# Attention and FFN in one kernel: the first two chunks take turns in the FFN, three inner tiles each and then thirteen each

## The chip, the cores and the metric

The kernel runs on one core of one Trainium2 chip. The metric is the device time of one execution in microseconds (us); less is better. Engines are named as in the profile: PE is the matrix engine (PEld its weight loads), DVE VectorE, ACT ScalarE, POOL GpSimd, SP SyncE, which here only issues DMAs.

## The reference

Attention over blocks of 32 queries, each seeing 16 keys to its left, 8 to its right and 8 memory keys; its output, with the heads side by side, is the input x of an FFN with 3072 tokens, 512 model columns and 2048 inner units:

```python
scores = scale * np.matmul(q_c, k_full.transpose(0, 1, 3, 2))
a = np.exp(scores - np.max(scores, axis=-1, keepdims=True))
out[:, :, c_start:c_end] = np.matmul(a / (np.sum(a, axis=-1, keepdims=True) + 1e-09), v_full)

h = x @ w_in                      # x: attention's output, (3072, 512)
r = np.maximum(h, 0.0)
g = s * (r * r) + b               # s and b: one number each
return (g @ w_out).astype(np.float32)
```

## The kernel before, in words

The 3072 tokens are cut into 8 chunks of 384. Each chunk has an attention part (4 pairs of heads) and an FFN part of 16 steps, one for each tile f of 128 inner units. A step is `hidden(u)`, 12 matmuls that make h from x (L504), four ACT instructions (relu, square, affine, and the rounded high part gH, L511 to L514), one DVE instruction (the low part gL, L515), and `result(u)`, 9 matmuls that add g times w_out into three PSUM accumulators (L526). x, g and the weights are held as a high and a low fp32r part, so that a product is three matmuls.

The weights come as 64-bit numbers, 512 KB for each of the 32 weight tiles (w_in and w_out, 16 each, "half" 0 and 1). Each is decoded once, in `weight`: ACT scales the upper word (L481), DVE shifts the lower word (L482), joins the two (L484) and puts the sign in (L486), ACT rounds the high part (L490) and DVE subtracts to get the low part (L491). The raw words lie in ten tiles `early0` to `early9`, and after these in a ring `words` of four tiles; the joined number lies in a ring `wv` of three. A tile of `words` can be loaded again once L486 has read it.

One pair of heads in attention: scores (PE, L377), row maxima with the mask (DVE, L434, eight to a pair), exp (ACT, L438, eight), a reciprocal (DVE, L443) and a multiplication (POOL, L444) for each of the two heads, then a turn: for the first two chunks PE transposes (L453) and ACT or DVE copies (L456, L458), for later chunks DVE transposes in 32x32 blocks (L464). The values product (L409) and the two parts of x (ACT L413, DVE L414) end it. Tiles `t` and `aT` are rings of four, two to a pair of heads.

The order of the FFN steps is the list `STEPS`: eight steps of chunk 0 (f 0 to 7), sixteen of chunk 1, the other eight of chunk 0, then chunks 2 to 7. At a change of chunk the three accumulators are put aside (`result`, L537, ACT) and added to later (L544, DVE).

The order on each engine is not written by hand: `Plan.lay` (L140) is a list scheduler over all operations, with a due time for each (a weight: `ORDER`, L50; a pair of heads: `anchor`, L346), a table of durations (`HOLD`), and a model of the DMAs (`RATE`, `LAND`, at most eight in flight). What it lays is the in-order program of each engine; the wait for a late operand holds everything behind it on that engine. While PE has nothing to do in the first 40 us, filler matmuls are laid (L304). s and b are loaded by two small DMAs, one number to each of 128 partitions (L310, L311).

Of the kernel before, what the change touches and what calls it, by code (L numbers as in the profile page):

```python
# [11 lines left out]
F32 = mybir.dt.float32  # L12
# [27 lines left out]
NEG = -2.0 ** 100  # L40
NEARLY = 16
NTURN = 2
N0 = 8
LAG = 2
NALONE = 2
JOIN = 2.0
APART = 3.0
LEAD = 3.5
BANKS = 8
ORDER = sorted((f + half, half, f) for f in range(NF) for half in range(2))  # L50
LATE_W = [x[1:] for x in ORDER[-NEARLY:]]

STEPS = ([(0, f) for f in range(N0)] + [(1, f) for f in range(NF)] + [(0, f) for f in range(N0, NF)]
         + [(ch, f) for ch in range(2, NCHUNK) for f in range(NF)])


HOLD = dict(hidden=535, result=712, scores=306, turn=84, value=254, warm=215, group=1900, group1=1230,
            relu=388, square=388, affine=570, high=388, xhigh=388, wscale=571, whigh=536, copy=270, exp=386, keep=388, store=480, bias=500,  # L60
            low=475, affine_v=475, rec=120, max=212, flip=316, xlow=470, wlow=345, wjoin=610, wsign=612, out=600,
            small=240, norm=1010, wrest=1290, issue=440)
LATE = dict(PE=230, ACT=180, DVE=180, POOL=150, SP=0)
RATE, LAND = 400.0, 2000.0
FLIGHT = 8
BEGIN = dict(PE=2500.0, ACT=2500.0, DVE=2500.0, POOL=2500.0, SP=800.0)

# [46 lines left out]
class Plan:  # L114
# [25 lines left out]
    def lay(self, filler=None):  # L140
# [8 lines left out]
        waiting = {e: [] for e in engines}  # L149
        ready = {e: [] for e in engines}  # L150
        events = sorted(BEGIN.values())
        wire, flying = 0.0, []
        laid = []
        back = []
        for o in self.ops:
# [3 lines left out]
        while todo:  # L159
            t = heapq.heappop(events)  # L160
            while events and events[0] <= t:
                heapq.heappop(events)
            while back and back[0][0] <= t:
                v = heapq.heappop(back)[-1]
                v.ring.back(v)
            for e in engines:
                while waiting[e] and waiting[e][0][0] <= t:
                    o = heapq.heappop(waiting[e])[2]
                    heapq.heappush(ready[e], (o.prio, o.n, o))
                if free[e] > t:  # L170
                    continue
                if e == "SP":
                    flying = [x for x in flying if x > t]
                    if len(flying) >= FLIGHT:
                        heapq.heappush(events, min(flying))
                        continue
                put, got = [], None
                while ready[e]:
                    x = heapq.heappop(ready[e])
                    o = x[2]  # L180
                    new = [v for v in o.vals if v.slot is None and v.ring.tiles is not None]
                    other = "POOL" if e == "DVE" else "DVE"
                    held = o.lock and e in lock and lock[other] > t

                    if o.lock and e in lock and free[other] <= t and any(y[2].lock and y[:2] < x[:2] for y in ready[other]):
                        put.append(x)
                        continue
                    given = []
                    for v in new if not held else ():
                        if not v.ring.can(v):  # L190
                            break
                        v.ring.give(v)
                        given.append(v)
                    if not held and len(given) == len(new):
                        got = o
                        break
                    for v in reversed(given):
                        v.ring.undo(v)
                    if held:
                        heapq.heappush(events, lock[other])  # L200
                    put.append(x)
                for x in put:
                    heapq.heappush(ready[e], x)
                if got is None:
                    if e == "PE" and filler and filler[0](t):
                        laid.append((t, -1, filler[1]))
                        free[e] = t + HOLD["warm"]
                        heapq.heappush(events, free[e])
                    continue
                o = got  # L210
                o.start = t
                free[e] = t + o.hold
                o.end = free[e] + LATE[e]
                if o.size:
                    wire = max(wire, t) + o.size / RATE
                    o.end = wire + LAND
                    flying.append(o.end)
                if o.lock and e in lock:
# [22 lines left out]


@with_exitstack
def body(ctx: ExitStack, tc: tile.TileContext, qkv, w1, w2, s_in, b_in, out):
    nc = tc.nc
    plan = Plan()
    op = plan.op
# [9 lines left out]


    wts = {}
    early = [const.tile([P, 2 * DM], F32, name=f"early{i}", tag=f"slot{i}") for i in range(NEARLY)]  # L260

    def weight_tile(half, f):
        if (half, f) not in wts:
# [8 lines left out]
    xr = [[const.tile([P, TOK], F32R, name=f"x{a}{c}_{i}") for a in "HL" for c in range(NC_T)] for i in range(2)]  # L272
    x_ring = Ring(xr)
    wvs = ring("wv", 3, [P, DM], F32)
    words = ring("words", 4, [P, 2 * DM], F32)
    raws = ring("raw", 2, [P, QK], F32)
    ts_ = ring("t", 4, [QB, GB, P], F32)
    vs_ = ring("v", 2, [P, 2 * GB * D], F32)
    aTs = ring("aT", 4, [P, GB, QB], F32)
    stats = Ring([tuple(const.tile([QB, GB], F32, name=f"{n}{i}") for n in ("nmax", "den", "rden")) for i in range(4)])  # L280
    gs = Ring([(const.tile([P, TOK], F32R, name=f"gH{i}"), const.tile([P, TOK], F32R, name=f"gL{i}")) for i in range(3)])
    outs = ring("partial", 3, [P, DM], F32)

    spare = [BANKS - 1]

# [21 lines left out]
    c_id, c_aT, c_mask, c_s, c_b = (fixed() for _ in range(5))  # L307
    op("ACT", "copy", -100, lambda: nc.scalar.activation(s_sb, ones[:, :1], AF.Exp), (), (c_s[0],))
    op("POOL", "copy", -100, lambda: make_identity(nc, ident), (), (c_id[0],))
    op("SP", "issue", -8, lambda: nc.sync.dma_start(s_sb, s_in.to_broadcast([P, 1])), (), (c_s[0],), size=64)  # L310
    op("SP", "issue", -8, lambda: nc.sync.dma_start(b_sb, b_in.to_broadcast([P, 1])), (), (c_b[0],), size=64)  # L311

    def constants():
        for x in aTs.tiles:
            nc.gpsimd.memset(x, 0.0)
# [16 lines left out]
    class Early:  # L332


        def __init__(self, i, lo, hi):
            self.val, self.lo, self.tile = c_early[i], lo, early[i][:, lo:hi]

        def __getitem__(self, key):
            return self.val[self.lo, key]
# [6 lines left out]
    def anchor(ch, c):  # L346
# [1 line left out]
        if ch == 0:  # L348
            return -30 + 2 * c
        if ch < NALONE:  # L350
            return starts[ch] - LEAD - 2.0 * (H // 2 - 1 - c)
        return starts[ch] - JOIN - (4.0 if ch > NALONE else APART) * (H // 2 - c)

    x_vals, open_ = {}, []
# [1 line left out]
    def attend(ch, c):  # L356
# [9 lines left out]
            v = Early(NEARLY - 5 - c // 2, c % 2 * DM, (c % 2 + 1) * DM)  # L366
        t, aT = [Val(ts_) for _ in range(2)], [Val(aTs) for _ in range(2)]
        due = a if alone else anchor(ch, c + 1)
        op("SP", "issue", a - 4, lambda: nc.sync.dma_start(raw.tile, qkv[b, half, c, :, :QK]), (), (raw[0],), size=P * QK * 4)
        op("SP", "issue", due - 1.5, lambda: nc.sync.dma_start(v.tile, qkv[b, half, c, :, QK:]), (), (v[0],), size=P * 2 * GB * D * 4)  # L370
        scv = lambda n: scs[n].tile[:QB].rearrange("q (j k) -> q j k", j=GB)

        def product(j):
# [97 lines left out]
    def weight(i, half, f, due):  # L471
# [13 lines left out]
           (raw["lo"],), (v[0],), lock=True)  # L485
        op("DVE", "wsign", due, lambda: nc.vector.scalar_tensor_tensor(bits(), hi(), -2147483648, bits(), ALU.bitwise_and, ALU.bitwise_or),  # L486
           (raw["hi"],), (v[0],), lock=True)
        rest = half or f >= N0
# [29 lines left out]
    def result(u):  # L518
# [9 lines left out]
        for t in range(NT):  # L528
# [6 lines left out]
            if f < NF - 1:  # L535
                o = partial[t] = Val(outs)
                op("ACT", "store", u, lambda acc=acc, o=o: nc.scalar.activation(o.tile, acc.tile, AF.Copy), (acc[0],), (o[0],))  # L537
                continue
            o = partial[t] if not ch else Val(wvs if ch == 1 else outs)
            ot = lambda o=o: o.tile  # L540
            if ch:
                op("DVE", "out", u, lambda acc=acc, ot=ot: nc.vector.tensor_copy(ot(), acc.tile), (acc[0],), (o[0],))
            else:
                op("DVE", "out", u, lambda acc=acc, ot=ot: nc.vector.tensor_tensor(ot(), acc.tile, ot(), ALU.add), (acc[0],), (o[0],))  # L544
            row = ch * TOK + t * P
            op("SP", "issue", u, lambda ot=ot, row=row: nc.sync.dma_start(out[row:row + P, :], ot()), (o[0],), (), size=P * DM * 4)

# [61 lines left out]
```

## Time and profile before

| | us |
|---|---|
| three runs | 645.0, 645.26, 648.97 (median 645.26) |
| the profiled execution | 644.32 |
| its span, from the first instruction to the last | 642.5 |
| PE busy | 626.1 (97%) |
| DVE busy | 356.8 (56%) |
| ACT busy | 422.2 (66%) |
| POOL busy | 87.7 (14%) |

The span is 1.8 us shorter than the execution it was taken from. A busy share is a mean over the whole span; a window shows what one stage is limited by. In the timeline a number in brackets is the time that the engine stood idle before the instruction, with the one that released it. Durations of neighbours on DVE and ACT overlap a little in the records, so what an instruction costs in a full queue is the distance from its start to the next start.

### The profile page before, as it was taken

To read this page: it belongs to the slowest core of one execution; us is meant where nothing else is said; L and a number is where in the kernel's file an instruction comes from. 1 tells how busy PE (TensorE), PEld (TensorE's weight loads), DVE (VectorE), ACT (ScalarE), POOL (GpSimd) and SP (SyncE) were. 2 spreads that over 40 slices of the span, in tenths; PEclk is the share of its full clock that TensorE was granted. 3 is DMA by queue.
4 is the path that set the end of the run, shared out by engine and by line. 5 is a ranking of instruction groups with operands and counts; after the bars stand their busy time and mean duration, and the time that the engine had idled before them with its cause. 6 is when DMAs were issued, how large, how long until landed. Compare 5 with 4: busy or idle time off the path is not lost.

```text
span 642.5 us, 10812 instructions
## 1 busy us (share of the span) xinstructions
PE 626.1 (97%) x3818; PEld 545.1 (85%) x3822; DVE 356.8 (56%) x1283; ACT 422.2 (66%) x1137; POOL 87.7 (14%) x138
## 2 busy tenths in 40 slices
PE   9899988999999999999999999999999999999997
PEld 5578877888888988888898988889888888989995
DVE  4899999816667355573447554473555734421112
ACT  6799998656766466666556566664666665555543
POOL 3622200101221011110011111110111100100000
PEclk9999999999999999999999999999999999999999
DMA  8933654002212011121002111120111200010001
GB/s 285 408 140 99 231 199 169 1 9 75 103 46 95 1 45 46 46 95 46 19 27 95 46 45 46 46 96 0 46 46 46 95 17 2 1 49 1 1 0 50
DMA packets 17622, 46.83 MB, mean 73 GB/s; under 512 B 2208, under 2 KB 2208, under 8 KB 17568
## 3 DMA queue, kind: packets, MB, share of 16 engines
q1 hardware_dynamic: 17568, 46.15, 20.5%
q8 instruction: 30, 0.49, 0.3%
q14 instruction: 24, 0.20, 0.1%
HBM read 39.85 MB, written 6.29 MB: 72 GB/s over the span
## 4 chain that ended last, share of the span: by engine, by line
PE 79%; ACT 8%; DVE 8%; DMA 2%; issue 1%; POOL 0%; SPq 0%; DVEq 0%; POOLq 0%; ACTq 0%
PE ps L526 37%; PE ps L504 36%; PE ps L377 4%; PE ps L409 3%; ACT t L438 2%; DVE wv L484 2%; ACT wv L481 1%; DVE wv L486 1%; DVE w L491 1%; ACT w L490 1%; DMA early<-w 1%; DMA early<-qkv 1%; ACT ps L513 1%; DVE gL L515 1%; DVE words L482 1%
## 5 line engine op out<-in xcount | busy, mean ns | idle before, releaser
L504 PE MATMUL ps<-xH,w 128*128 128x384 f32 x1024 | 261.8, 337 | 0.5 <-DVE w L491 0.5
L526 PE MATMUL ps<-w,gH 128*128 128x512 f32 x768 | 239.8, 393 | 0.0
L504 PEld LDWEIGHTS ps<-xH,w 128*128 128x128 f32 x1024 | 186.0, 188 | 7.0 <-DVE w L491 1.8
L511 ACT ACTIVATE ps<-ps 128x384 f32<-128x384 f32 x128 | 60.9, 475 | 184.4 <-PE ps L504 184.3
L504 PE MATMUL ps<-xL,w 128*128 128x384 f32 x512 | 174.2, 340 | 0.0
L526 PEld LDWEIGHTS ps<-w,gH 128*128 128x128 f32 x768 | 144.2, 188 | 28.1
L526 PE MATMUL ps<-w,gL 128*128 128x512 f32 x384 | 155.0, 404 | 7.4 <-DVE gL L515 7.4
L515 DVE TENSOR_TENSOR gL<-ps,gH 128x384 fp32r<-128x384 f32 x128 | 70.7, 552 | 146.7 <-ACT gH L514 144.5
L464 DVE STREAM_TRANSPOSE aT<-t 32x128 f32<-32x128 f32 x384 | 116.2, 303 | 51.1 <-POOL t L444 46.4
L438 ACT ACTIVATE t<-t,nmax 96x128 f32<-96x128 f32 x256 | 99.6, 391 | 10.4 <-DVE nmax L434 5.3
L504 PEld LDWEIGHTS ps<-xL,w 128*128 128x128 f32 x512 | 96.1, 188 | 6.2 <-DVE xL L414 0.2
L434 DVE CUSTOM_DVE_ANT_0 t<-ps,mask 96x128 f32<-96x128 f32 x256 | 58.6, 282 | 69.4 <-PE ps L377 69.0
L526 PEld LDWEIGHTS ps<-w,gL 128*128 128x128 f32 x384 | 72.0, 187 | 25.2 <-DVE gL L515 10.0
L444 POOL TENSOR_TENSOR t<-t,rden 96x512 f32<-96x512 f32 x64 | 68.4, 1069 | 131.6 <-DVE rden L443 131.6
L513 ACT ACTIVATE ps<-ps,b_sb,s_sb 128x384 f32<-128x384 f32 x128 | 82.5, 645 | 4.2
L514 ACT ACTIVATE gH<-ps 128x384 fp32r<-128x384 f32 x128 | 62.9, 492 | 3.9
L512 ACT ACTIVATE ps<-ps 128x384 f32<-128x384 f32 x128 | 60.8, 475 | 4.0
L441 POOL TENSOR_SCALAR rden<-den 96x4 f32<-96x4 f32 x64 | 17.2, 268 | 332.6 <-ACT t L438 329.9
L438 ACT ACTIVATION_READ_ACCUMULATOR t<-t,nmax 96x1 f32 x256 | 48.3, 189 | 0.0
L377 PE MATMUL ps<-raw 64*96 64x128 f32 x448 | 32.3, 280 | 0.0
L377 PEld LDWEIGHTS ps<-raw 64*96 64x96 f32 x448 | 25.4, 159 | 4.7 <-issue 1.1
L409 PEld LDWEIGHTS ps<-aT,v 128*64 128x64 f32 x448 | 20.0, 136 | 8.4 <-issue 6.8
(43 smaller groups left out, 290.0 us busy)
## 6 DMA issues: line engine op xcount, KB each, us to landing
raw<-qkv SPq DMA_DIRECT2D x28, 448.0 KB, 3.4
words<-w SPq DMA_DIRECT2D x22, 512.0 KB, 4.1
v<-qkv SPq DMA_DIRECT2D x28, 256.0 KB, 3.6
out<-partial SPq DMA_DIRECT2D x21, 256.0 KB, 2.1
early<-w SPq DMA_DIRECT2D x10, 512.0 KB, 9.3
early<-qkv SPq DMA_DIRECT2D x4, 448.0 KB, 5.5
early<-qkv SPq DMA_DIRECT2D x4, 256.0 KB, 7.4
out<-wv SPq DMA_DIRECT2D x3, 256.0 KB, 4.5
```

The lines of the kernel that those rows point to most:

```text
L377: nc.tensor.matmul(scv(n)[:, j, :], raw.tile[rows, j * QB:(j + 1) * QB], raw.tile[rows, TOK + j * P:TOK + (j + 1) * P], start=True, stop=True)
L434: op("DVE", "max", a + 0.1, lambda j=j: nc.vector.tensor_tensor_reduce(t.tile[:, j, :], scv()[:, j, :], mask[:, kind(j)], -SCALE, 3.0e38, ...
L438: op("ACT", "exp", a + 0.2, lambda j=j: nc.scalar.activation(t.tile[:, j, :], t.tile[:, j, :], AF.Exp, bias=nmax()[:, j:j + 1], scale=-1.0 ...
L444: op("POOL", "norm", a + 0.25, lambda: nc.gpsimd.tensor_tensor(t.tile, t.tile, rden().unsqueeze(2).to_broadcast([QB, GB, P]), ALU.mult), [ ...
L464: nc.vector.transpose(aT.tile[gg, :, cs], t.tile[cs, :, gg])
L504: nc.tensor.matmul(h.tile[:, :TOK], weight_tile(0, f)[:, wi, c * P:(c + 1) * P], x.tile[xi], start=(c == 0 and n == 0), stop=(c == NC_T - ...
L511: op("ACT", "relu", u, lambda: nc.scalar.activation(hp(), hp(), AF.Relu), (), (h[0],))
L512: op("ACT", "square", u, lambda: nc.scalar.activation(hp(), hp(), AF.Square), (), (h[0],))
L513: op("ACT", "affine", u, lambda: nc.scalar.activation(hp(), hp(), AF.Identity, scale=s_sb, bias=b_sb), (c_s[0], c_b[0]), (h[0],))
L514: op("ACT", "high", u, lambda: nc.scalar.activation(g.tile[0], hp(), AF.Copy), (h[0],), (g["H"],))
L515: op("DVE", "low", u, lambda: nc.vector.tensor_tensor(g.tile[1], hp(), g.tile[0].bitcast(F32), ALU.subtract), (h[0], g["H"]), (g["L"],))
L526: nc.tensor.matmul(acc.tile, g.tile[gi][:, t * P:(t + 1) * P], weight_tile(1, f)[:, wi, :], start=(first and n == 0), stop=(last and n == 2))
```

## The change

`STEPS` becomes: chunk 0 with f 0 to 2, chunk 1 with f 0 to 2, chunk 0 with f 3 to 15, chunk 1 with f 3 to 15, then chunks 2 to 7. The due time of a weight follows the first step that uses it. Both chunks keep partial sums, so the ring `partial` has six tiles and `words` three. s and b stand as two more columns in the array of q, k and v (a row is 1410 numbers and was 1408); the first load brings them, and POOL copies them out. The scheduler's table has a longer `group`, and its DMA model a lower rate for the first six loads.

```diff
-N0 = 8
+SECOND = 1.0
-ORDER = sorted((f + half, half, f) for f in range(NF) for half in range(2))
+PARTS = [0, 3, NF]
+STEPS = ([(ch, f) for lo, hi in zip(PARTS, PARTS[1:]) for ch in range(2) for f in range(lo, hi)]
+         + [(ch, f) for ch in range(2, NCHUNK) for f in range(NF)])
+FIRST = {}
+for _u, (_, _f) in enumerate(STEPS):
+    FIRST.setdefault(_f, _u)
+ORDER = sorted((FIRST[f] + half, half, f) for f in range(NF) for half in range(2))
-STEPS = ([(0, f) for f in range(N0)] + [(1, f) for f in range(NF)] + [(0, f) for f in range(N0, NF)]
-         + [(ch, f) for ch in range(2, NCHUNK) for f in range(NF)])
...
 RATE, LAND = 400.0, 2000.0
+SLOW, NSLOW = 290.0, 6
...
-                    wire = max(wire, t) + o.size / RATE
+                    wire = max(wire, t) + o.size / (RATE if sent >= NSLOW else SLOW)
+                    sent += 1
...
-    words = ring("words", 4, [P, 2 * DM], F32)
+    words = ring("words", 3, [P, 2 * DM], F32)
...
-    outs = ring("partial", 3, [P, DM], F32)
+    outs = ring("partial", 2 * NT, [P, DM], F32)
...
-    op("SP", "issue", -8, lambda: nc.sync.dma_start(s_sb, s_in.to_broadcast([P, 1])), (), (c_s[0],), size=64)
-    op("SP", "issue", -8, lambda: nc.sync.dma_start(b_sb, b_in.to_broadcast([P, 1])), (), (c_b[0],), size=64)
...
-            return starts[ch] - LEAD - 2.0 * (H // 2 - 1 - c)
+            return starts[ch] - LEAD - SECOND * (H // 2 - 1 - c)
...
+            first = early_tiles[NEARLY - 1][:, :QK + 2]
+            op("SP", "issue", a - 4, lambda: nc.sync.dma_start(first, qkv[b, half, c, :, :QK + 2]), (), (raw[0],), size=P * QK * 4)
+            op("POOL", "small", -25, lambda: nc.gpsimd.tensor_copy(s_sb, first[:, QK:QK + 1]), (raw[0],), (c_s[0],))
+            op("POOL", "small", -25, lambda: nc.gpsimd.tensor_copy(b_sb, first[:, QK + 1:]), (raw[0],), (c_b[0],))
...
+    sb = np.broadcast_to(np.stack([moe_s.reshape(()), moe_b.reshape(())]), q2.shape[:-1] + (2,))
-        "qkv": np.concatenate([q2, k2, v2], axis=-1),
+        "qkv": np.concatenate([q2, k2, sb, v2], axis=-1),
```

The scheduler lays another order on every engine. On SP, at the end of the loads of chunk 0, this stood before (s, b, a weight, then the first pair of chunk 1):

```order
L370 DMA early10_71<-qkv 128x512 x2
L310 DMA s_sb_78<-s_in 128x1
L311 DMA b_sb_79<-b_in 128x1
L479 DMA early0_61<-w1 128x1024
L369 DMA raw0_104<-qkv 128x896
L479 DMA early1_62<-w1 128x1024
```

and this stands there now:

```order
L380 DMA early10_71<-qkv 128x512 x2
L373 DMA raw0_103<-qkv 128x896
L373 DMA raw1_104<-qkv 128x896
L489 DMA early0_61<-w1 128x1024
L380 DMA v0_109<-qkv 128x512
L489 DMA early1_62<-w1 128x1024
```

Two pairs of chunk 1 now load ahead of the first weight. On DVE, where the first two weights are shifted, this stood before (t2 with nmax2, in the last rows, is the fourth pair of chunk 0):

```order
L434 ISA nmax1_119 96x1
L482 TENSOR_SCALAR early0_61<-early0_61 128x512
L443 RECIPROCAL rden3_127<-rden3_127 96x4
L482 TENSOR_SCALAR early1_62<-early1_62 128x512
L458 COPY aT2_114<-ps6_143 128x384
L414 TENSOR_TENSOR xL0_0_85<-ps3_140,xH0_0_81 128x384
L434 ISA t2_108,nmax2_122<-ps1_138,mask_80 96x128
```

and this stands there now:

```order
L444 ISA t3_108,nmax3_124<-ps2_141,mask_80 96x128
L444 ISA nmax3_124 96x1
L453 RECIPROCAL rden1_120<-rden1_120 96x4
L492 TENSOR_SCALAR early0_61<-early0_61 128x512
L468 COPY aT0_111<-ps5_144 128x384
L424 TENSOR_TENSOR xL1_0_86<-ps0_139,xH1_0_82 128x384
L453 RECIPROCAL rden2_123<-rden2_123 96x4
L492 TENSOR_SCALAR early1_62<-early1_62 128x512
```

The shifts moved behind the fourth pair's maxima. Later on DVE, from the sign of one weight in a tile of `words` (first row), this stood before:

```order
L486 SCALAR_TENSOR_TENSOR wv2_99<-words0_100,wv2_99 128x512
L491 TENSOR_TENSOR w0_13_1198<-wv1_98,w0_13_1198 128x512
L515 TENSOR_TENSOR gL0_129<-ps4_141,gH0_128 128x384
L491 TENSOR_TENSOR w1_12_1211<-wv2_99,w1_12_1211 128x512
L482 TENSOR_SCALAR words1_101<-words1_101 128x512
L484 SCALAR_TENSOR_TENSOR wv0_97<-wv0_97,words1_101 128x512
L486 SCALAR_TENSOR_TENSOR wv0_97<-words1_101,wv0_97 128x512
L482 TENSOR_SCALAR words2_102<-words2_102 128x512
L484 SCALAR_TENSOR_TENSOR wv1_98<-wv1_98,words2_102 128x512
L486 SCALAR_TENSOR_TENSOR wv1_98<-words2_102,wv1_98 128x512
L491 TENSOR_TENSOR w0_14_1240<-wv0_97,w0_14_1240 128x512
L515 TENSOR_TENSOR gL1_131<-ps0_137,gH1_130 128x384
```

and this, at the tightest place, stands there now, where the last row shifts the next weight in the same tile:

```order
L496 SCALAR_TENSOR_TENSOR wv1_98<-words0_100,wv1_98 128x512
L492 TENSOR_SCALAR words1_101<-words1_101 128x512
L492 TENSOR_SCALAR words2_102<-words2_102 128x512
L453 RECIPROCAL rden0_117<-rden0_117 96x4
L524 TENSOR_TENSOR gL0_128<-ps4_143,gH0_127 128x384
L500 TENSOR_TENSOR w0_7_970<-wv1_98,w0_7_970 128x512
L494 SCALAR_TENSOR_TENSOR wv2_99<-wv2_99,words1_101 128x512
L496 SCALAR_TENSOR_TENSOR wv2_99<-words1_101,wv2_99 128x512
L492 TENSOR_SCALAR words0_100<-words0_100 128x512
```

Seven rows stand between the sign and the next shift of one tile, where with four tiles more than eleven stood.

## Rows read from the trace of the kernel before

**Rows 1.** Windows: length; busy (instructions) of PE, PEld, DVE, ACT, POOL; PEclk, DMA share, GB/s.

```profile
30.00:40.00 10.00, 9.93 (x76) 7.82 (x74) 9.59 (x22) 9.87 (x27) 2.95 (x4) 1.00 0.68 263
...
90.00:100.00 10.00, 8.80 (x43) 7.45 (x42) 9.62 (x18) 8.77 (x17) 0.00 (x0) 1.00 0.65 212
100.00:110.00 10.00, 8.62 (x42) 7.22 (x41) 9.59 (x18) 8.06 (x16) 0.00 (x0) 1.00 0.59 202
...
120.00:140.00 20.00, 20.00 (x102) 17.95 (x101) 7.99 (x23) 10.52 (x21) 1.25 (x2) 1.00 0.00 0
```

**Rows 2.** Timeline of PE: the last result that waits in the decoding, and the third after it.

```profile
115.71 0.50 PE L526 MATMUL ps<-w,gL 128*128 128x512 f32 x1 [0.89 <-DVE gL L515]
...
128.40 0.39 PE L526 MATMUL ps<-w,gL 128*128 128x512 f32 x1
```

**Rows 3.** Groups of PE, 28 to 116 us: busy, mean ns | idle before, releaser.

```profile
L526 PE MATMUL ps<-w,gL 128*128 128x512 f32 x43 | 17.9, 417 | 6.0 <-DVE gL L515 6.0
```

**Rows 4.** Windows of L515 alone: gL made by 118.6 us.

```profile
0.00:118.60 118.60, 8.84 (x16) 1.00 0.58 207
```

**Rows 5.** Timeline of DVE, one period of the decoding.

```profile
93.81 0.55 DVE L515 TENSOR_TENSOR gL<-ps,gH 128x384 fp32r<-128x384 f32 x1
94.28 0.68 DVE L491 TENSOR_TENSOR w<-wv,w 128x512 fp32r<-128x512 f32 x1
94.88 0.42 DVE L482 TENSOR_SCALAR words<-words 128x512 int32<-128x512 int32 x1
95.34 0.69 DVE L484 SCALAR_TENSOR_TENSOR wv<-wv,words 128x512 int32<-128x512 int32 x1
96.06 0.69 DVE L486 SCALAR_TENSOR_TENSOR wv<-words,wv 128x512 int32<-128x512 int32 x1
96.67 0.43 DVE L482 TENSOR_SCALAR words<-words 128x512 int32<-128x512 int32 x1
...
99.14 0.55 DVE L515 TENSOR_TENSOR gL<-ps,gH 128x384 fp32r<-128x384 f32 x1
```

**Rows 6.** Timeline of DVE, the end of the decoding.

```profile
117.97 0.55 DVE L515 TENSOR_TENSOR gL<-ps,gH 128x384 fp32r<-128x384 f32 x1
118.44 0.16 DVE L443 RECIPROCAL rden<-rden 96x4 f32<-96x4 f32 x1
118.52 0.26 DVE L434 CUSTOM_DVE_ANT_0 t<-ps,mask 96x128 f32<-96x128 f32 x1
...
118.70 0.28 DVE L434 CUSTOM_DVE_ANT_0 t<-ps,mask 96x128 f32<-96x128 f32 x1
...
120.19 1.87 DVE L464 STREAM_TRANSPOSE aT<-t 32x128 f32<-32x128 f32 x6
```

**Rows 7.** Timeline of DVE, its waits for the first weights.

```profile
15.80 0.43 DVE L482 TENSOR_SCALAR early<-early 128x512 int32<-128x512 int32 x1 [2.33 <-DMA early<-w]
...
18.20 0.43 DVE L482 TENSOR_SCALAR early<-early 128x512 int32<-128x512 int32 x1 [1.89 <-DMA early<-w]
```

**Rows 8.** Waits of 0 to 30 us: total, times, longest.

```profile
POOL rden L441 <- ACT t L438: 5.1, 1, 5.1
...
ACT t L438 <- DVE rden L443: 3.2, 1, 3.2
```

**Rows 9.** Timeline of ACT, one exp and the next.

```profile
20.64 0.39 ACT L438 ACTIVATE t<-t,nmax 96x128 f32<-96x128 f32 x1
21.03 0.39 ACT L438 ACTIVATE t<-t,nmax 96x128 f32<-96x128 f32 x1
```

**Rows 10.** Timeline of SP, issues 13 to 20 (each waits for a landing).

```profile
13.39 0.33 SPq L369 DMA_DIRECT2D raw<-qkv  x1
14.53 0.33 SPq L370 DMA_DIRECT2D v<-qkv  x1
15.79 4.00 SPq L479 DMA_DIRECT2D early<-w  x4
```

**Rows 11.** Tile words, 55 to 118 us: its loads, issue to landing.

```profile
DMA to landing us min/median/max: 3.0/3.7/4.7
```

More of the change, by code (lines that the diff above doesn't have):

```diff
@@ L49 @@
 BANKS = 8
-ORDER = sorted((f + half, half, f) for f in range(NF) for half in range(2))
+PARTS = [0, 3, NF]
[5 more added lines that the diff above has]
+ORDER = sorted((FIRST[f] + half, half, f) for f in range(NF) for half in range(2))
 LATE_W = [x[1:] for x in ORDER[-NEARLY:]]
-STEPS = ([(0, f) for f in range(N0)] + [(1, f) for f in range(NF)] + [(0, f) for f in range(N0, NF)]
-         + [(ch, f) for ch in range(2, NCHUNK) for f in range(NF)])
-HOLD = dict(hidden=535, result=712, scores=306, turn=84, value=254, warm=215, group=1900, group1=1230,
+HOLD = dict(hidden=535, result=712, scores=306, turn=84, value=254, warm=215, group=2060, group1=1230,
             relu=388, square=388, affine=570, high=388, xhigh=388, wscale=571, whigh=536, copy=270, exp=386, keep=388, store=480, bias=500,
@@ L151, in lay @@
         events = sorted(BEGIN.values())
-        wire, flying = 0.0, []
+        wire, flying, sent = 0.0, [], 0
         laid = []
@@ L243, in body @@
 @with_exitstack
-def body(ctx: ExitStack, tc: tile.TileContext, qkv, w1, w2, s_in, b_in, out):
+def body(ctx: ExitStack, tc: tile.TileContext, qkv, w1, w2, out):
     nc = tc.nc
@@ L259, in body @@
     wts = {}
-    early = [const.tile([P, 2 * DM], F32, name=f"early{i}", tag=f"slot{i}") for i in range(NEARLY)]
+    early_tiles = [const.tile([P, 2 * DM], F32, name=f"early{i}", tag=f"slot{i}") for i in range(NEARLY)]
     def weight_tile(half, f):
@@ L335, in __init__ @@
         def __init__(self, i, lo, hi):
-            self.val, self.lo, self.tile = c_early[i], lo, early[i][:, lo:hi]
+            self.val, self.lo, self.tile = c_early[i], lo, early_tiles[i][:, lo:hi]
         def __getitem__(self, key):
@@ L368, in attend @@
         due = a if alone else anchor(ch, c + 1)
-        op("SP", "issue", a - 4, lambda: nc.sync.dma_start(raw.tile, qkv[b, half, c, :, :QK]), (), (raw[0],), size=P * QK * 4)
-        op("SP", "issue", due - 1.5, lambda: nc.sync.dma_start(v.tile, qkv[b, half, c, :, QK:]), (), (v[0],), size=P * 2 * GB * D * 4)
+        if ch or c:
+            op("SP", "issue", a - 4, lambda: nc.sync.dma_start(raw.tile, qkv[b, half, c, :, :QK]), (), (raw[0],), size=P * QK * 4)
+        else:
+            first = early_tiles[NEARLY - 1][:, :QK + 2]
+            op("SP", "issue", a - 4, lambda: nc.sync.dma_start(first, qkv[b, half, c, :, :QK + 2]), (), (raw[0],), size=P * QK * 4)
+            op("POOL", "small", -25, lambda: nc.gpsimd.tensor_copy(s_sb, first[:, QK:QK + 1]), (raw[0],), (c_s[0],))
+            op("POOL", "small", -25, lambda: nc.gpsimd.tensor_copy(b_sb, first[:, QK + 1:]), (raw[0],), (c_b[0],))
+        op("SP", "issue", due - 1.5, lambda: nc.sync.dma_start(v.tile, qkv[b, half, c, :, QK + 2:]), (), (v[0],), size=P * 2 * GB * D * 4)
         scv = lambda n: scs[n].tile[:QB].rearrange("q (j k) -> q j k", j=GB)
@@ L487, in weight @@
            (raw["hi"],), (v[0],), lock=True)
-        rest = half or f >= N0
         old = list(c_early[LATE_W.index((half, f))].parts.values()) if (half, f) in LATE_W else []
@@ L534, in result @@
                 continue
-            if f < NF - 1:
-                o = partial[t] = Val(outs)
+            o = partial.get((ch, t))
+            if f < NF - 1 and o is None:
+                o = partial[ch, t] = Val(outs)
                 op("ACT", "store", u, lambda acc=acc, o=o: nc.scalar.activation(o.tile, acc.tile, AF.Copy), (acc[0],), (o[0],))
                 continue
-            o = partial[t] if not ch else Val(wvs if ch == 1 else outs)
+            o = o or Val(outs)
             ot = lambda o=o: o.tile
-            if ch:
+            if ch > 1:
                 op("DVE", "out", u, lambda acc=acc, ot=ot: nc.vector.tensor_copy(ot(), acc.tile), (acc[0],), (o[0],))
@@ L544, in result @@
                 op("DVE", "out", u, lambda acc=acc, ot=ot: nc.vector.tensor_tensor(ot(), acc.tile, ot(), ALU.add), (acc[0],), (o[0],))
+            if f < NF - 1:
+                continue
             row = ch * TOK + t * P
@@ L591 @@
     v2 = windows(v, mem_v).reshape(B, H // 2, 2, HALVES, GB, P, D).transpose(0, 3, 1, 5, 2, 4, 6).reshape(B, HALVES, H // 2, P, 2 * GB * D)
+    sb = np.broadcast_to(np.stack([moe_s.reshape(()), moe_b.reshape(())]), q2.shape[:-1] + (2,))
     arrays = {
-        "qkv": np.concatenate([q2, k2, v2], axis=-1),
+        "qkv": np.concatenate([q2, k2, sb, v2], axis=-1),
         "w1": np.ascontiguousarray(moe_w_in.reshape(NC_T, P, NF, P).transpose(2, 1, 0, 3)).view(np.int64),
         "w2": np.ascontiguousarray(moe_w_out).view(np.int64),
-        "s_in": np.ascontiguousarray(moe_s).reshape(1, 1),
-        "b_in": np.ascontiguousarray(moe_b).reshape(1, 1),
     }
@@ L605 @@
     with tile.TileContext(nc) as tc:
-        body(tc, args[0], w1, w2, *args[3:], out)
+        body(tc, args[0], w1, w2, out)
     r = run_bass_kernel_spmd(nc, [arrays], core_ids=[0])
```

## The prediction

> **What bounds the kernel now.** I read the busy shares of the page first: PE 97%, so what can be won lies where PE waits. Then I cut the span into windows [rows 1]. From 120 us on PE is busy for 20.00 of 20.00 us and DVE for 7.99: there the kernel is bound by PE. Before that it is the other way round: in the window from 90 us DVE is busy for 9.62 of 10 us, ACT for 8.77 and PE for 8.80, and from 30 us DVE and ACT are both full (9.59 and 9.87). This first stage holds attention of the first two chunks and the decoding of all 32 weight tiles, which is never done again. So the kernel is a stage bound by DVE and ACT, and after it a queue of PE work that no longer waits. The time is set by how many FFN steps PE has behind it when the first stage lets it go.
>
> That point can be dated. In the timeline of PE a result waits 0.89 us for gL at 115.71 us [rows 2]; results before it waited in the same way, 6.0 us between 28 and 116 us [rows 3]. The windows of the gL line alone count 16 of them by 118.6 us [rows 4], so gL of step 15 is the one that starts at 117.97 [rows 6], and the result at 115.71 is that of step 14. From there PE runs through: the result of step 17 starts at 128.40 [rows 2], which is 12.69 us for three steps, 4.23 us a step. In the timeline of DVE between two gL of 93.81 and 99.14 us there stand two decoded weights and nothing else, 5.33 us [rows 5]. The program before lets chunk 0 and chunk 1 use the first weights, so at step 15 all but one weight half are decoded though only f 0 to 7 have been used: DVE decoded f 8 to 15 early, and PE waited for gL queued among them.
>
> **The change part by part.** I count in the order of DVE what stands ahead of a given gL, before and now, and date gL of step 17 in the new program; what PE has left after the result of step 17 is the same work in both.
>
> *The order of the steps.* Ahead of gL 15 in the old order and ahead of gL 17 in the new one stand the same 32 shifts, joins and signs, the same 31 subtractions and the same copies. The new one has in addition 2 gL, 5 block transposes, 3 row maxima and 1 reciprocal. By start-to-start distances these are 0.47 us for a gL (117.97 to 118.44), 0.08 for a reciprocal, 0.18 for a maximum, and 1.87/6 = 0.31 for a transpose [rows 6]: 0.94 + 1.55 + 0.54 + 0.08 = 3.1 us. gL 15 ended at 118.44, so with nothing else changed gL 17 ends at 121.5, and its result starts about 0.1 us later (the record of a gL lasts 0.55 us, 0.08 beyond the next start [rows 5, 6]): 121.6 against 128.40, a gain of 6.8 us. In words: two steps of PE work more (8.5 us) are done for 3.1 us more on DVE, because in steps 6 to 18 the decoding serves steps that use each weight as it comes.
>
> ACT has to follow. Up to the same points it gains 2 steps, 3 stores of accumulators and 3 exps. A step costs it about 2.2 us (10.52 us of the 20 from 120 us, in which 4.7 steps lie [rows 1]), an exp 0.39 [rows 9], a store about a gL's 0.55 (an estimate): 4.4 + 1.7 + 1.2 = 7.3 us. What covers it is idle time of ACT: 1.23 and 1.94 us in the two windows from 90 us [rows 1], and 3.2 us in the first 30 us, where it waited for DVE [rows 8], 6.4 us in these alone. That nearly covers it. I cost it at 0 and keep 0 to +2.
>
> *The start.* At 15.80 and 18.20 us DVE stands before the shifts of the first two weights, 2.33 and 1.89 us [rows 7], 4.2 us in which the maxima of the fourth pair are queued behind; ACT's 3.2 us are their consequence [rows 8]. In the new order these shifts stand behind those maxima. The loads of s and b go too: issue 16 waits for the landing of the s load, issue 17 for that of b, issue 18 for the first weight, at 13.39, 14.53 and 15.79 us [rows 10], so these two loads of 0.5 KB hold 1.1 to 1.3 us of the queue each, as much as the 512 KB behind them (1.26). Without them the 0.9 MB of two raw tiles that now go first leave the first weight about where it was. What is late next is ACT: ahead of its first gH now stand 17 more exps (60 for 43), 4 copies and 2 xH more: 17 at 0.39 [rows 9] and 6 at about 0.45 (an estimate) are 9.3 us, against 3.2 us no longer waited; ahead of DVE's first gL stand 17 maxima, 5 reciprocals and 2 xL more, some 4.5 us by [rows 6]. So in the worst case DVE waits 9.3 - 3.2 - 4.5 = 1.6 us for ACT and wins nothing; at best all 4.2 us go. Ends: -4.2 and +1.6. I take -2.5, nearer to the two waits since they have rows.
>
> *s and b on POOL.* Two copies of one column. POOL idles 5.1 us ahead of its first reciprocal [rows 8], so they are hidden; uncovered they would cost less than a reciprocal's 0.16 us each. 0.
>
> *The row of 1410 numbers.* No row here shows a load whose rows start off a round address. The loads that matter are the twelve of attention that go out early, 4.1 MB; at 512 KB in 1.26 us [rows 10] they take some 10 us, and a tenth more or less of that would be 1 us. I take 0 and keep both ends. The Trainium skill, "DMA: Bandwidth & Descriptors", "How a descriptor splits into AXI transactions", says that a descriptor which does not start at a multiple of 256 B takes a transaction more: here 15 for 14 in a raw row and 9 for 8 in a row of v. By that rule these loads would take about 8% longer, an estimate of 0.8 us, and the sum would be 637.8 and not 637.0.
>
> *Three tiles for words.* SP issues the next load when DVE has put the sign in, and DVE comes to the next shift of that tile when it has done what stands between. At the tightest place that is two shifts, a reciprocal, a gL, a subtraction, a join and a sign: 0.92 + 0.08 + 0.47 + 0.60 + 0.72 + 0.61 = 3.4 us by [rows 5, 6] (0.46 for a shift). Counted in the same way the 19 reuses have 3.4 to 7.2 us, and only four have less than 4.6. With four tiles the distance is over 8 us in the steady stretch. A load takes 3.0 to 4.7 us, 3.7 in the median [rows 11], and DVE shows no wait for one there. At 3.3 us nothing is lost; at 4.6 us the four tight places lose 1.2 + 0.7 + 0.4 + 0.1 = 2.4 us. I take 1.0; ends 0 and 2.4.
>
> *The rest.* Six stores and six additions in place of three and three, and copies to `partial`: off the path, since after 120 us DVE is idle for 60% [rows 1]. The longer `group` moves attention of later chunks by fractions of a step, beside a PE that is full. 0.
>
> **Sum.** 121.6 - 2.5 + 1.0 = 120.1 us for the result of step 17, 8.3 us ahead of 128.40. The span becomes 642.5 - 8.3 = 634.2 and the profiled execution 644.32 - 8.3 = 636.0. The median of the runs lies 0.9 above that execution, so I predict 645.26 - 8.3 = 637.0 us. PE sets a floor: it waited 6.0 us for gL in the stage [rows 3], and what it can win beyond that must come from a start that is earlier, so I expect nothing much over 11 us.
>
> **The rivals.** A measurement of this kernel can tell 1%, 6.5 us, from no change.
>
> *The front is paced by ACT.* Chunk 1's attention now stands ahead of nearly all weights, ACT is full from 30 us on [rows 1], and its 7.3 us more are not covered. Then the start gives nothing back (+1.6 in place of -2.5) and the word tiles cost their 1.0: 121.6 + 1.6 + 1.0 = 124.2 us for that result, a gain of 4.2: 641.1 us, within 1%. For it speaks ACT's 9.87 of 10; against it that ACT has 3.2 us of waiting at the start to give.
>
> *DVE waits for the words at nearly every weight: slower.* The place is the shift of each of the 19 weights that reuse a tile. If a load took 6.0 us from sign to shift, the shortfalls add up to about 17 us, the result of step 17 would start at 119.1 + 17 = 136.1, 7.7 us later than before: 653 us. It decides against the change from about 5.4 us on, where the stalls reach 9.3 us. Against it: the longest load in the stretch took 4.7 [rows 11]; for it: loads are then issued closer to their use, and each wait holds gL behind it. The Trainium skill, "Perfetto Trace Analysis", "Optimization Strategy", reads an even row of gaps on the engine that should be full as a sign of too few buffers; no run here shows it yet, since there were four tiles.
>
> *The turn doesn't bring the steps nearer*: chunk 1's x comes late, PE stands before step 3 for it, and DVE has no gL to make. It would have to come 8.3 us late to undo the gain, 645.3 us. In DVE's order its last xL stands five rows ahead of gL of step 2, so DVE would be held little longer than PE; I give this little.
>
> **How the numbers follow.** The forecast 0.63, with a range of its own from 633.5 to 638.8; paced by ACT 0.26; words 0.06; the late turn 0.05. Faster by over 1% is the forecast: 0.63. Slower by over 1% is the words rival: 0.06. Within 1% are the other two: 0.31. The lower end is all of 4.2 won at the start and no wait for words, a gain of 11.0, with 0.8 for the spread of runs: 633.5. The upper end is the ACT rival with word waits of 2.4, a gain of 2.8: 642.5.
>
> **What would show it.** Right: the last result of PE that waits for gL in a row of waits is that of step 17 or 18, at about 120 us, and PE is full after; no DVE wait for `early` at the start; DVE waits for `words` of about 1 us in all; the two loads of 0.5 KB that held the queue for over a microsecond each are gone. Wrong: the result of step 17 later than 122 us; DVE waits for `words` over 3 us; or PE waits that reappear after step 19, which would mean that its remaining work is not the same.

## The result, and the profile after

| | before | after |
|---|---|---|
| median of six runs each, us | 645.21 | 639.36 (638.72 to 641.63) |
| the profiled execution, us | 644.32 | 639.74 |
| its span, us | 642.5 | 638.0 |

The ratio is 0.990, with a 95% interval of 0.9875 to 0.9925: 5.85 us or 0.9% faster, some 2.4 us less than forecast. Between the two profiled executions it is 4.58 us; the median of before lies 0.89 above its profiled execution and that of after 0.38 below, which makes up the rest.

The windows of after that answer to [rows 1] (length; busy of PE, PEld, DVE, ACT, POOL; PEclk, DMA share, GB/s):

```profile
90.00:100.00 10.00, 10.00 (x53) 9.18 (x52) 9.63 (x19) 8.94 (x17) 0.00 (x0) 1.00 0.47 161
100.00:110.00 10.00, 8.97 (x45) 7.51 (x44) 9.17 (x18) 8.36 (x17) 0.00 (x0) 1.00 0.57 190
```

In the decoding PE has become fuller (10.00 and 8.97 for 8.80 and 8.62), with DVE about as full as it was (9.63 and 9.17 for 9.62 and 9.59).

The timeline of PE in after, where [rows 2] stood for before, shows the first row of results 16 and 17:

```profile
120.62 0.50 PE L535 MATMUL ps<-w,gL 128*128 128x512 f32 x1 [0.74 <-DVE gL L524]
...
124.90 0.39 PE L535 MATMUL ps<-w,gL 128*128 128x512 f32 x1
```

The result of step 17 starts at 124.90, where before had 128.40: 3.5 us gained and not 8.3. The last wait for gL in the row is that of step 16. Up to 130 us PE waits 4.1 us for gL (total, times, longest), where before has 6.0:

```profile
PE ps L535 <- DVE gL L524: 4.1, 7, 0.9
```

So the steps come closer, as forecast. What went the other way is seen in the timeline of DVE. The first gL in before:

```profile
36.42 0.55 DVE L515 TENSOR_TENSOR gL<-ps,gH 128x384 fp32r<-128x384 f32 x1
```

and in after, the first gL and, where [rows 6] stood, that of step 17:

```profile
44.05 0.56 DVE L524 TENSOR_TENSOR gL<-ps,gH 128x384 fp32r<-128x384 f32 x1 [0.25 <-ACT gH L523]
...
123.80 0.56 DVE L524 TENSOR_TENSOR gL<-ps,gH 128x384 fp32r<-128x384 f32 x1
```

The first gL comes 7.6 us later (36.42 to 44.05). The prediction's own terms put it at 38.4: 36.42, 4.5 for the attention work that now stands ahead of it on DVE, and -2.5 for the start. From there to gL of step 17 it takes 79.75 us, where before took 90.21 (126.63 - 36.42). The steps are faster and the start is slower.

DVE's waits up to its first gL (total, times, longest), in before from 6 to 37 us:

```profile
DVE early L482 <- DMA early<-w: 4.2, 2, 2.3
DVE t L434 <- PE ps L377: 3.4, 1, 3.4
DVE rden L443 <- POOL rden L441: 0.8, 2, 0.5
DVE aT L458 <- PE ps L453: 0.6, 1, 0.6
```

and in after from 6 to 45 us, where no wait for `early` is left:

```profile
DVE t L444 <- PE ps L387: 4.7, 3, 4.1
DVE rden L453 <- POOL rden L451: 3.4, 4, 1.2
DVE aT L468 <- PE ps L463: 2.6, 4, 0.9
```

The 4.2 us of [rows 7] did go, as forecast. In their place DVE waits 5.9 us more for POOL and PE; 0.7 of that is the first maximum, which starts at 6.43 us and not at 5.73. In after SP's issues, where [rows 10] stood, show no load that holds the queue for its 0.5 KB: the weights run on from 11.05 us.

```profile
11.05 5.81 SPq L489 DMA_DIRECT2D early<-w  x6
```

### The profile page after: what moved, and what is told of

Its sections match the earlier page's. It is cut to its first block, busy times and chain, and to the rows that moved or that the text cites. A ratio compares the mean times of both kernels' runs of the same rounds, so it can differ in the third digit from the quotient of the medians.

```text
span 638.0 us, 10874 instructions
## 1 busy us (share of the span) xinstructions
PE 626.8 (98%) x3831; PEld 546.0 (86%) x3835; DVE 355.6 (56%) x1283; ACT 422.8 (66%) x1140; POOL 88.2 (14%) x140
## 4 chain that ended last, share of the span: by engine, by line
PE 83%; ACT 7%; DVE 4%; DMA 3%; issue 1%; POOL 1%; SPq 0%; DVEq 0%; ACTq 0%; POOLq 0%
PE ps L535 37%; PE ps L513 36%; PE ps L387 4%; PE ps L419 4%; ACT wv L491 1%; DMA early<-w 1%; ACT w L499 1%; DVE wv L494 1%; DVE w L500 1%; PE ps L310 1%; ACT t L448 1%; ACT ps L522 1%; DMA early<-qkv 1%; PE ps L463 1%; ACT ps L521 1%
## 5 line engine op out<-in xcount | busy, mean ns | idle before, releaser
L444 DVE CUSTOM_DVE_ANT_0 t<-ps,mask 96x128 f32<-96x128 f32 x256 | 56.5, 281 | 5.1 <-PE ps L387 4.7
```

Source lines behind the costliest of these rows:

```text
L444: op("DVE", "max", a + 0.1, lambda j=j: nc.vector.tensor_tensor_reduce(t.tile[:, j, :], scv()[:, j, :], mask[:, kind(j)], -SCALE, 3.0e38, ...
```

## The experiments

In the expectations "theory S", "theory L" and "theory D" stand for: the start is held by the fillers ahead of the scores; the gain comes from the loads of s and b; the gain comes from the due times of the weights, not from the turn.

### What holds the start: fillers and loads

The first run is after unaltered, on another chip.

> The changed kernel unaltered, as the mark for the runs beside it. All theories: 638.7 to 640 us, 5 to 6.5 us under the kernel before; the result of step 17 at 124 to 125 us; the first gL at 44 us.

Measured: 639.41 us, ratio 0.9891 (0.9864 to 0.9919). The result stands.

Then 32 of after's fillers were left out, those laid behind the first values product of chunk 0, and in another kernel, with `fillers[:2]` in place of `fillers[KEEP:]`, two of the first nine:

```diff
+KEEP = 27
...
+    fillers = [x for x in laid if x[1] < 0]
+    skip = {id(x) for x in fillers[KEEP:]}
-        for _, _, fn in laid:
-            fn()
+        for x in laid:
+            if id(x) not in skip:
+                x[2]()
```

> The changed kernel without its last 32 filler matmuls (those behind the first values product of chunk 0); the order is otherwise the same. Theory S (the start is late because PE runs through fillers that were laid into gaps which are not there): the first gL comes at 41 to 42.5 us in place of 44.0, the result of step 17 1.5 to 3 us sooner, 636.5 to 638 us. Rival A (the start is paced by ACT, which is full from its first exp on): first gL within 0.5 us of 44.0, time within 0.7 us of the unaltered one. Against both: the granted clock falls below 1.00 where the fillers are gone, and the time is the same or up to 3 us longer.

> The changed kernel without two of the nine filler matmuls ahead of the first scores (there were seven before). Theory S and rival A alike: the first maximum on DVE at 5.7 us in place of 6.43, the first exp at 6.1 in place of 6.76, the first gL 0.5 to 0.7 us sooner, 0.4 to 0.8 us in the total. If the start hangs on neither PE nor ACT but on the weights' loads, nothing moves: within 0.2 us.

Measured: 641.12 us (0.9913, interval 0.9888 to 0.9939) without the late fillers, 639.22 (0.9885, 0.986 to 0.991) without the two early ones. From the first exp to the first gL it takes 37.29 us in after (44.05 - 6.76), 37.30 in its repeat, 37.45 without the late fillers and 37.29 without the two early ones. In before it takes 30.36 (36.42 - 6.06). The first exps of the two, in the timelines of ACT:

```profile
6.06 0.40 ACT L438 ACTIVATE t<-t,nmax 96x128 f32<-96x128 f32 x1 [3.83 <-DVE nmax L434]
...
6.76 0.40 ACT L448 ACTIVATE t<-t,nmax 96x128 f32<-96x128 f32 x1 [4.54 <-DVE nmax L444]
```

The first exp itself moves: it is at 5.63 in the unaltered repeat and at 5.53 without the two early fillers, so what these two are worth cannot be told. The late fillers do not hold the start, and theory S is out. They have another use. The windows without them:

```profile
20.00:30.00 10.00, 6.69 (x78) 5.00 (x78) 8.64 (x47) 10.00 (x46) 7.29 (x9) 0.96 1.03 408
30.00:40.00 10.00, 10.00 (x91) 8.45 (x90) 8.46 (x41) 9.09 (x31) 4.23 (x6) 0.87 0.71 238
```

PE is busy for 6.69 of 10 us (9.78 in after), and the granted clock is 0.96 of 2.4 GHz in that stretch and 0.87 in the one behind, so part of them ran at the lower level of 1.2 GHz; in after it is 1.00 in both. By the medians the kernel is 1.7 us slower than the repeat of after, as the third case of the expectation had it. The traced execution is not: it took 639.73 us, its span is 638.0 as in after, and its gL of step 17 starts at 123.79. The mean granted clock of the other five, 0.991 to 0.995, is lower than its 0.996, and 0.999 to 1.000 in the repeat; that the clock makes up the 1.7 us is likely and not shown.

### The three tiles for words

After in its exact order, with four tiles behind the names of three:

```diff
+    words.more = words.tiles + [const.tile([P, 2 * DM], F32, name="words3")]
...
-        return self.ring.tiles[self.slot]
+        more = self.ring.more
+        return more[self.phys % len(more)] if more else self.ring.tiles[self.slot]
```

> The changed kernel with four tiles behind the ring of three that the order was made with: the order on every engine is the same, only a load no longer waits for the sign three weights back. Theory W (the third tile was worth its wait): DVE's 0.9 us and ACT's 0.8 us of waits for words are gone and the result of step 17 comes 0.8 to 1.7 us sooner. Rival: these waits lie where ACT or DVE wait for each other anyway, under 0.4 us.

Measured: 638.54 us (0.9877, 0.985 to 0.9904), 0.87 below the repeat of after. DVE waits for `words` 0.9 us in after and not at all here; gL of step 17 starts at 123.07 and not at 123.80. The term was priced at 1.0 and measures 0.7 in the trace and 0.9 by the medians, whose intervals overlap.

### The parts of the change, one at a time

On the kernel before: s and b in the first load; the due times alone; the turn with the due times; and the due times with s and b in the first load. The diff shows the edit of s and b (first and fourth kernel), of the due times (second to fourth) and of the turn (third).

```diff
-    op("SP", "issue", -8, lambda: nc.sync.dma_start(s_sb, s_in.to_broadcast([P, 1])), (), (c_s[0],), size=64)
-    op("SP", "issue", -8, lambda: nc.sync.dma_start(b_sb, b_in.to_broadcast([P, 1])), (), (c_b[0],), size=64)
...
+        "qkv": np.concatenate([q2, k2, sb, v2], axis=-1),
...
-ORDER = sorted((f + half, half, f) for f in range(NF) for half in range(2))
...
+FIRST = {}
+for _u, (_, _f) in enumerate(STEPS):
+    FIRST.setdefault(_f, _u)
+ORDER = sorted((FIRST[f] + half, half, f) for f in range(NF) for half in range(2))
...
+PARTS = [0, 3, NF]
+STEPS = ([(ch, f) for lo, hi in zip(PARTS, PARTS[1:]) for ch in range(2) for f in range(lo, hi)]
...
+    words = ring("words", 3, [P, 2 * DM], F32)
...
+    outs = ring("partial", 2 * NT, [P, DM], F32)
```

> The kernel before with s and b in the first pair's load alone; the order on PE, ACT and DVE is that of before. Theory L (the two small loads hold the loads behind them by 2.4 us, and the start of the old order hangs on the first weights): DVE's two waits for them (4.2 us) shrink to 1.5 to 2.5, the first gL comes at 34 to 35 in place of 36.4, the total falls by 1.8 to 2.5 us, about 643. Rival: the start hangs on ACT, under 0.5 us.

> The kernel before, steps in the old order (8, 16, 8), with the new rule alone by which a weight is due at the first step that uses it. Theory D (what counts is that DVE decodes no weight ahead of a gL that PE waits for; the turn is one means to it): ahead of the last weight now stand 19 gL in place of 16; gL of step 17 at 123 to 124 us, the total 4 to 5.5 us lower, 640 to 641. Rival T (the turn itself gives the steps): the gain is under 2 us, above 643.

> The kernel before with the turn alone: steps 3, 3, 13, 13 with their dues, six partial tiles and three for words; s and b as before, the old anchors and the old load rate in the scheduler. Theory T: the gain of the whole change less what s and b bring, 3.5 to 5.5 us, 640 to 642. Theory D: the same gain, since it has the same dues. Against both: if the s and b loads make up most of the change, under 2 us.

> The two together on the kernel before: old steps, new dues, s and b in the first load, four tiles for words. Theory D with L: the gains add, 6 to 7.5 us, 638 to 639.5, as good as the whole change without the turn. Rival: they overlap, since PE is full from 60 us on in either: 4.5 to 5.5 us.

| kernel | steps | due times | s, b | median us | ratio, interval |
|---|---|---|---|---|---|
| before (20 runs) | 8, 16, 8 | old | two loads | 645.51 | |
| s and b | 8, 16, 8 | old | first load | 642.81 | 0.9953 (0.9933 to 0.9973) |
| due times | 8, 16, 8 | new | two loads | 640.96 | 0.9938 (0.9918 to 0.9957) |
| turn and due times | 3, 3, 13, 13 | new | two loads | 644.01 | 0.9984 (0.9966 to 1.0002) |
| due times, s and b | 8, 16, 8 | new | first load | 637.34 | 0.9879 (0.9862 to 0.9897) |

This shows where the gain comes from. By the medians s and b give 2.7 us, the due times 4.5, and the two together 8.2, where their sum is 7.2 and 6 to 7.5 were expected. The kernel with both is at least as good as after without any turn: its runs (636.90 to 638.48) lie below all twelve of after (638.59 to 641.63), though after ran on other chips and has one tile less for words.

The turn gives nothing. Both theories expected 640 to 642 us for it with the due times; it measured 644.01 (642.17 to 646.66), 3.0 behind the due times alone. Not all of that is the turn: this kernel has three tiles for words, and in its trace PE waits 2.8 us for a tile of `raw` at 33.81 us, with a granted clock of 0.83 from 30 to 40 us. The closest comparison is after with four tiles for words, 0.9877 of before on its chip, against the old steps with due times and s and b, 0.9879: no difference. The longer `group`, `SECOND` and the lower load rate of the scheduler were not tried alone.

What the due times do stands in PE's waits up to 130 us (total, times, longest). With old due times and s and b in the first load:

```profile
PE ps L530 <- DVE gL L519: 6.1, 6, 2.2
```

with new due times alone:

```profile
PE ps L529 <- DVE gL L518: 1.6, 2, 1.0
```

Most of the waits of [rows 3] go without any turn: 6.0 us become 1.6, and the 4.4 won are the size of the gain. Four of the six in before lay 5.3 us apart and lasted 0.88 or 0.89 each, one for every two weights decoded. While chunk 1 uses f 0 to 7 for the second time no new weight is needed; the old rule decoded f 8 to 15 at the pace of f + half, as if it were, and gL queued among them.

One expectation was missed here. The gL of step 17 was to come at 123 to 124 us and came at 126.37, and the traced execution took 642.79, 1.8 above the median of its kernel. In this trace the start is late: the first gL comes at 39.37 and not at 36.42, DVE waits 5.8 us for the first weights (4.2 in before), and the granted clock is 0.83 from 20 to 30 us. From the first gL to that of step 17 it takes 87.00 us where before has 90.21. With s and b in the first load the due times shorten that stretch from 91.70 to 87.28 us, by 4.4. What s and b do stands in DVE's waits of the first kernel, up to 130 us:

```profile
DVE gL L519 <- ACT gH L518: 4.4, 4, 3.0
...
DVE early L486 <- DMA early<-w: 1.2, 1, 1.2
```

The waits for the first weights fall from 4.2 to 1.2 us and the first gL comes at 34.00, 2.4 earlier. The hole that the two loads leave is in the DMA rate: in the three us from 10 on it is 149, 164 and 238 GB/s in before, and 413, 431 and 416 here. That is the -2.5 of the forecast, but in the old order. What is late next is ACT's gH, as the forecast feared: of the 2.4 us, 0.9 are left at gL of step 17 (125.70 for 126.63), and the traced execution is 1.0 us faster than that of before, less than the medians say.

The kernel with both has its first gL and that of step 17 here, in the timeline of DVE:

```profile
33.81 0.56 DVE L522 TENSOR_TENSOR gL<-ps,gH 128x384 fp32r<-128x384 f32 x1
...
121.09 0.55 DVE L522 TENSOR_TENSOR gL<-ps,gH 128x384 fp32r<-128x384 f32 x1
```

87.28 us lie between them, against 79.75 with the turn. So the turn, with one tile less for words, wins 7.5 us in the steps and pays 10.2 for it at the start (44.05 - 33.81).

### Which engine paces the start

The constant 37.3 us say that the start is set by the order, not yet by which engine. In after's order some work of chunk 1 was done twice: eight ACT copies in one kernel, sixteen row maxima on DVE in another.

```diff
-            op("ACT", "keep", a + 0.3, lambda: nc.scalar.activation(aT.tile, keep(), AF.Copy), ready, (aT[0],))
+            op("ACT", "keep", a + 0.3, lambda: [nc.scalar.activation(aT.tile, keep(), AF.Copy) for _ in range(act)], ready, (aT[0],))
...
+            weights(a + n * 0.5, half * GB, scs[n], t[n], st[n], lambda n=n: scv(n), 2 if ch == 1 and n == 0 else 1)
...
+                t.tile[:, j, :], scv()[:, j, :], mask[:, kind(j)], -SCALE, 3.0e38, ALU.add, ALU.min, nmax()[:, j:j + 1]) for _ in range(again)],
```

> The kernel after in its exact order, with each of the eight ACT copies of chunk 1's turned tiles made twice (the second repeats the first; 6 more stand ahead of the first gH, about 0.45 us each, 2.7 us). Theory ACT (the front is a queue of ACT's work from the first exp on): the first gL comes 39.5 to 40.3 us after the first exp, not 37.3. Theory DVE or PE (ACT has slack there): 37.3 to 38.0.

> The kernel after in its exact order, with the sixteen row maxima of the first head of each pair of chunk 1 made twice on DVE (the second repeats the first; all 16 stand ahead of the first gL, 0.18 us each, 2.9 us). Theory ACT: DVE has waits there that take most of it, the first gL comes 37.3 to 38.5 us after the first exp. Theory DVE: 39.7 to 40.3. If both this and the run with doubled copies come 2 us later, the front is bound by both in turns.

Measured, one execution each: first gL 38.85 us after the first exp with the copies doubled (44.95 - 6.10), 41.45 with the maxima doubled (47.86 - 6.41); 642.92 and 643.32 us. In the timelines a doubled copy takes 0.89 to 0.91 us from start to start and not 0.39, so 6 of them add 3.1, of which 1.55 arrive. A doubled maximum takes 0.54 and not 0.21, so 16 add 5.3, of which 4.15 arrive. Neither theory holds by itself, and both numbers lie outside the stretches that were given for them. Half of what is added to ACT comes through and four fifths of what is added to DVE, though DVE is idle for longer. The waits from 16 to 48 us tell why. POOL and ACT in after:

```profile
POOL t L454 <- DVE rden L453: 5.7, 12, 0.9
```

```profile
ACT aT L466 <- PE ps L463: 1.0, 2, 0.8
```

and with the maxima doubled:

```profile
POOL t L454 <- DVE rden L453: 10.1, 11, 2.1
```

```profile
ACT aT L466 <- PE ps L463: 3.5, 4, 1.4
```

A reciprocal that stands behind more maxima on DVE comes later; POOL multiplies later, PE turns later, ACT waits for the turned tile, and the time it loses there it lacks for the exps behind. With the copies doubled ACT shows no wait in that stretch, so there it is full. So the start is a loop over four in-order engines with ACT nearly full in it (19.13 of 20 us from 16 to 36 us in after).

### The place of the turn

After with four tiles for words, the old distance between chunk 1's pairs, and the turn at eight or five tiles:

```diff
-SECOND = 1.0
+SECOND = 2.0
...
-PARTS = [0, 3, NF]
+PARTS = [0, 8, NF]
...
-    words = ring("words", 3, [P, 2 * DM], F32)
+    words = ring("words", 4, [P, 2 * DM], F32)
```

> The kernel after with turns of eight and eight tiles in place of three and thirteen, the old distance of 2.0 between chunk 1's pairs, and four tiles for words; due times and the load of s and b as in the kernel after. Theory that the early turn costs the start: chunk 1's attention stands behind the first gL again, the first gL comes 27 to 29 us after the first exp, and the time is 636.5 to 638.0, as with due times and s and b alone (637.34). Theory that the turn at three has a use of its own: 639 or more.

> As the run with the turn at eight, but the turn at five tiles (five each, then eleven each). Theory that the early turn costs the start and gives back as much in the steps behind it: between 637.0 and 638.5, the first gL 31 to 35 us after the first exp. Theory that an early turn is best: no slower than 637.

Measured: 637.10 us at eight (0.9882, 0.9849 to 0.9915), 640.13 at five (0.9924, 0.9897 to 0.9951); the first gL comes 27.1 and 33.6 us after the first exp, both as expected. At eight, chunk 1's attention stands behind the first gL again and the time is that of the old steps with due times and s and b. So the turn at eight, which does not draw attention forward, costs nothing. The turn at five missed: it is slower than at three with four tiles (638.54), although its start is earlier, and its gL of step 18 is as early (127.32 against 127.31). Between the two traced executions it is 1.3 us (640.27 against 638.95), and 0.8 of that is a wait of PE for gL at 148.17 that the turn at three lacks; the rest was not found.

## Why the prediction was right and wrong

The time lies in the stated range, but a good part of that is the width of the range. The gain came out at 5.85 us for 8.3; at 0.9% it is not the gain of over 1% that had the chance of 0.63; 639.36 lies outside the forecast's own 633.5 to 638.8 and nearer to the ACT rival's 641.1 than to 637.0; and a sign that was named for being wrong came, the result of step 17 later than 122 us (124.90). The other signs came out as named: no DVE wait for `early`, 0.9 us of waits for `words`, the two small loads gone, and the last waiting result near 120 us, though it is that of step 16 and not 17 or 18. By its steps:

**The bound was read rightly.** PE waited for gL queued among early decoded weights, and those waits were what could be won: up to 130 us, 6.0 us became 4.1 in after and 1.6 with the due times alone.

**The order of the steps** came out better than its term. By the terms, from the first gL to that of step 17 it should have taken 81.1 us (119.5 - 38.4, where 119.5 is gL 15's 117.97 and 3.1, less 2.5, plus 1.0); it took 79.75. Its count of what stands ahead of gL 17 on DVE is exact in the trace of after. But the forecast took due times and turn for one thing, and gave the turn a gain that the due times bring without it. The change held both, so the gain came; as far as the turn goes, that is luck. Its sentence that decoding now serves steps that use each weight as it comes is right, and the due rule alone does that.

**The start is the term that failed**, in sign and beyond its upper end. It was priced at -2.5 within -4.2 and +1.6. Measured it is 7.6 - 4.5 = +3.1; 0.7 of that is a later first exp, which also moves between runs, and without it +2.4 are left. The working added up ACT's exps and copies and DVE's maxima and reciprocals, each engine for itself, and set the sums against DVE's waits as if they ran side by side. It left out POOL's multiplications and PE's transposes, and that all of these are steps of one loop over ACT, POOL, DVE and PE. The doubled copies and maxima showed that added work of either engine comes through, half of it on ACT and four fifths on DVE. "At best all 4.2 us go" was true of the wait for the weights and false of the time: 5.9 us of other waits replaced them.

**ACT must follow, at no cost**, held behind the start: DVE waits 1.1 us in all for gH up to 130 us. Of the rivals "the front is paced by ACT" came closest: 124.2 us forecast for the result of step 17, 124.90 measured. Its naming of one engine was half right: ACT is nearly full there, but DVE's added work delays the start too.

**Three tiles for words**: 1.0 forecast, 0.7 to 0.9 measured; from issue to landing loads to `words` took 3.1 to 4.7 us, 3.3 in the median, beside [rows 11].

The rival in which DVE waits at nearly every weight did not come: two waits, 0.9 us. By the Trainium skill, "Perfetto Trace Analysis", "Optimization Strategy", an even row of gaps on the engine that should be full can mean too few buffers; the trace shows no such row on DVE with three. The even row of 0.88 and 0.89 us that PE had in before was of another kind: it went with the due times, at the same number of tiles.

**The row of 1410 numbers**, at 0, held as far as the windows tell. From 3 to 9 us, where nearly all that moves is loads of attention, the DMAs moved 341 GB/s in after (346 in its repeat) and 334 in before; from 16 to 26 us, with weight loads among them, 406 and 409. The 8% that the prediction worked out from the rule in the Trainium skill, "DMA: Bandwidth & Descriptors", "How a descriptor splits into AXI transactions", does not show here (by the prediction's own counts it is 9%: 6 times 15 and 9 transactions for 6 times 14 and 8). A loss of a few per cent is not excluded.

**The rest.** The result of step 17 comes 3.5 us earlier and the span is 4.5 us shorter. Of the other 1.0, before has a wait of 0.58 us for gL at 166.77 that after lacks; the last 0.4 is not accounted for.

## What to carry to other kernels

Where a scheduler prepares data by due times, check that a due time follows the first use: preparing early on the engine that also makes the next step's operand cost 4.5 us here by the medians, and the waits name the operand that queues behind, not the early work. Price a move of work to the start along its whole loop of engines, not engine by engine: idle time of an engine inside such a loop is poor cover, as the doubled maxima showed. And try the parts of a change one at a time, since here two parts gave at least as much without the third.

## What was unexpected of the hardware

Two loads of 0.5 KB, 128 times one number, cost 2.7 us of the kernel's time together (1.7 to 4.3 by the interval), measured by taking them out alone; each held the queue for 1.1 to 1.3 us, as long as 512 KB, and the DMA rate fell to 149 GB/s beside them. Fillers that compute nothing of use were worth 1.7 us by the medians: without 32 of them the granted clock was 0.87 from 30 to 40 us. A copy on ACT that repeats the one ahead of it into the same tile took 0.52 us more, where the single one takes 0.39 from start to start, and a repeated maximum 0.33 more, where the single one takes 0.21.
